# A fused attention and feed-forward kernel: the last piece of q is cut at another row, and the last three blocks run their steps in another order

## The chip, the cores and the metric

The kernel runs on one core of a Trainium2 chip. The metric is device time in microseconds (us), the median of several executions; before the change it is 696.37 us (four runs, 696.32 to 696.72). One execution was also profiled.

The core's engines work side by side, each through its own queue of instructions in order: TensorE (PE in the profile, PEld for its weight loads) multiplies matrices into PSUM, VectorE (DVE) and ScalarE (ACT) work elementwise, GpSimd (POOL) here mostly issues transfers, SyncE (SP) issues transfers only. They wait for each other through semaphores.

## What is computed

Cross-covariance attention per batch (4 batches, 6080 tokens, 256 channels): q and k are normalised over the tokens, a 256 x 256 matrix of scores goes through a softmax, and its product with v passes through a feed-forward network with a hidden width of 2048 and the tanh form of GELU.

```python
def _attn_ref(q, k, v, tau):
    qn = q / (np.linalg.norm(q, axis=1, keepdims=True) + 1e-06)
    kn = k / (np.linalg.norm(k, axis=1, keepdims=True) + 1e-06)
    s = kn.transpose(0, 2, 1) @ qn / tau
    s = s - s.max(-1, keepdims=True)
    a = np.exp(s)
    a /= a.sum(-1, keepdims=True) + 1e-09
    return (v @ a).astype(np.float32)

def _moe_ref(x, w_in, w_out):
    h = x @ w_in
    c = np.float32(np.sqrt(2.0 / np.pi))
    g = 0.5 * h * (1.0 + np.tanh(c * (h + 0.044715 * h * h * h)))
    return (g @ w_out).astype(np.float32)
```

## The kernel before

**Start.** Batch 0's q and k come in six chunks of up to 8 rows (a row is 128 tokens of 256 channels). For each row TensorE adds to the Gram matrix of q and k (`gram_row`, L248) and to the sums of squares (`ss_rows`, L269 for q, L275 for k), of squares that ScalarE or VectorE forms (`square`, `square_rows`, L203 and L205). The last chunk is loaded in five transfers from POOL's queue, listed in `PIECES` as (0 for q or 1 for k, first row, row after the last). After it come eight filler matmuls (`warm`, L370), the transposition of the first block of v, and the scores (`scores`), from which the combined matrix aw = (attention times w_in) is formed.

**Blocks.** The tokens of all batches are cut into 48 blocks (n = 0 to 47) of 512 tokens; the last of each batch, so block 47 too, has 448. For a block, h = aw times v is formed, GELU gives g, and w_out times g is the output. Both products save multiplications with a scheme of sums and seven half-size products, so that many small sums stand between the matmuls. In a block of the last batch:

- `g0`, `g3`: plain products for pairs 0 and 3 of the hidden units (`mm1`, L521); `G0`, `G3` their GELU on ScalarE (L531).
- Three sets, 0 to 2, of the scheme for the first product. `w0m6` is product 6 of set 0 (`small`, L597). Its sums and GELUs are in `set_step`: `cq` and `y5` are copies on ScalarE (L613, L616), `ap` and `ax` sums on VectorE (L618, L621), `Gq`, `Gx`, `Gr` the GELUs (L623, L631, L628). Product m6 accumulates on the bank that `cq` reads, and m7 needs the sum `ap`.
- `vs`: sums of the next block's v (L559 to L562, VectorE).
- `T1a` to `T4b`: sums of g for the second product (L687, L699, L701, L703, VectorE); `M1A` to `M7B` are its products, four matmuls each (`product`, L726). They accumulate in two banks, r (M1, M6, M7, M4) and p (M5, M3, M2); in block 47 M2 has a bank s of its own.
- `cq`, `y5`, `y6` without a set: copies of r and p to SBUF on ScalarE (`keep`, L736). `ap`, `ax`, `c11a`, `a12`: sums on VectorE (L776, L742). `c11`, `c12`, `c21`, `c22`: transposition of the four quarters of the output on VectorE (`turn`, L751). `ax` reads r before M4 adds to it; `c11a` needs M2, `c21` M4, `c12` M3.
- A block is stored when its fourth quarter is turned (`store`, L816): four transfers from SP's queue, in block 46 two from SP and two from POOL. Block 47 is stored in halves (`store_half`, L804): `sB` after `c11` and `c21`, `sA` after `c12` and `c22`, each in two transfers from SP and two from ScalarE's queue, in turn.

**Order.** Nothing reorders these steps: `ORDER` is a list of strings, written out, and each engine's queue gets its instructions in the sequence of the steps. A suffix -1 or +1 means the block before or after. `WINDOW` gives each block its string; the last four strings serve blocks 44, 45, 46 and 47 alone.

```python
        for n in range(NN):
            for x in ORDER[WINDOW[n]].split():
                m = re.match(r"([A-Za-z]+\d*[A-Za-z]*\d?)(?:([+-])(\d+))?$", x)
                step(m[1], n + {None: 0, "+": 1, "-": -1}[m[2]] * int(m[3] or 0))
```

Transfers from SP and ScalarE signal through eight semaphores that the build deals out in turn; before a transfer uses one, its queue waits until the transfer that had it before has landed. Transfers from POOL have eight of their own.

Of the kernel before, what the change touches and what calls it, by code (L numbers as in the profile page):

```python
# [18 lines left out]
def kernel(  # L19
# [55 lines left out]
    def chunks_of(b):  # L75
        sizes = [8, 7, 8, 8, 8, 8] if b == 0 else [6, 6, 6, 6, 6, 6, 6, 5]
        assert sum(sizes) == R
        res, r0 = [], 0
        for n in sizes:
            res.append((r0, n))  # L80
            r0 += n
        return res
# [48 lines left out]

    PIECES = [(0, 0, 4), (1, 0, 5), (1, 5, 8), (0, 4, 6), (0, 6, 8)]

    def load_last():
        c = len(chunks_of(0)) - 1
# [2 lines left out]
        qk_tiles[0, c] = [qkp.tile([128, 8, 256], BF16, tag="qk"[w], name=f"last{w}") for w in range(2)]  # L140
        for w, a, e in PIECES:
            nc.gpsimd.dma_start(
# [26 lines left out]
    def rows_of(b, c):  # L169
        r0, n = chunks_of(b)[c]  # L170
        rows = [(r, 128) for r in range(n)]
        if with_rest(b, c):
            rows.append((n, REM))
        return rows

    def new_squares(b, c):
        sq = sqp.tile([128, 8, 512], BF16, tag="sq", name=f"sq{b}_{c}")
        if with_rest(b, c):
            nc.vector.memset(sq[REM:, chunks_of(b)[c][1], :], 0.0)
        SQ[b, c] = sq  # L180
# [16 lines left out]
    def square_rows(c, which, a, e, eng):  # L197
        if (0, c) not in SQ:
            new_squares(0, c)
        t = qk_tiles[0, c][which][:, a:e, :]  # L200
        o = SQ[0, c][:, a:e, which * 256 : which * 256 + 256]
        if eng == "act":
            nc.scalar.activation(o, t, AF.Square)  # L203
        else:
            nc.vector.tensor_mul(o, t, t)  # L205
# [34 lines left out]
    def gram_row(b, c, i):  # L240
        first = b not in G
        if first:
            G[b] = pM.tile([128, 2, 256], FP32, tag="a", name=f"G{b}")
        qt, kt = qk_tiles[b, c]
        rows = rows_of(b, c)
        r, np_ = rows[i]
        for jc in range(2):
            nc.tensor.matmul(  # L248
                G[b][:, jc, :],
                lhsT=qt[:np_, r, jc * 128 : jc * 128 + 128],  # L250
                rhs=kt[:np_, r, :],
                start=first and jc == 0, stop=jc == 1,
                skip_group_check=True)

    def ss_rows(c, which, rows=None):


        last = c == len(chunks_of(0)) - 1
        n = SQR.get((0, c), 8)
        rows = range(n) if rows is None else rows  # L260
        if c == 0:
            SS[which] = pM.tile([128, 2] if which == 0 else [128, 256], FP32,
                                tag="sp"[which], name=f"ss0{which}")
        sq = SQ[0, c]
        for r in rows:
            end = last and r == n - 1
            if which == 0:
                for jc in range(2):
                    nc.tensor.matmul(SS[0][:, jc : jc + 1],  # L269
                                     lhsT=sq[:, r, jc * 128 : jc * 128 + 128],  # L270
                                     rhs=ones_bf[:, 0:1],
                                     start=c == 0 and r == 0 and jc == 0,
                                     stop=end and jc == 1)
            else:
                nc.tensor.matmul(SS[1], lhsT=ones_bf, rhs=sq[:, r, 256:512],  # L275
                                 start=c == 0 and r == 0, stop=end)
# [544 lines left out]
    with tc.manual_schedule():  # L821
# [42 lines left out]
        c = nch - 1  # L864
# [6 lines left out]
        ss_rows(c, 0, range(0, 4))  # L871
        ss_rows(c, 1, range(0, 5))
        square_rows(c, 1, 5, 8, "dve")
        square_rows(c, 0, 4, 6, "dve")
        ss_rows(c, 1, range(5, 8))
        for i in (4, 5):
            gram_row(0, c, i)
        ss_rows(c, 0, range(4, 6))
        square_rows(c, 0, 6, 8, "dve")
        for i in (6, 7):  # L880
            gram_row(0, c, i)
        ss_rows(c, 0, range(6, 8))
        wi = moe_w_in.rearrange("(c p) d -> p c d", p=128)
        load_v0(0)
        for f0, f1 in ((0, 256), (256, 512), (512, 1024), (1024, 1536), (1536, 2048)):
# [293 lines left out]
    w1Gr T4b-1 w2m7 G3 w2m3 w2ax M2A-1 w2m2 ax-1 M2B-1 w2Gq T4a-1 w2m4""",  # L1179
    """g0 T1a-1 w2Gr-1 w1m1 G0 M4A-2 c11a-2 w0m5 w0m1 T3a-1 M4B-2 w0cq M5B-1 c21-2 w0y5 w1m5  # L1180
    T2a-1 w0m6 w2Gx-1 M5A-1 w0ap M1A-1 w1y5 M1B-1 T2b-1 w1cq w0m7 cq-1 w0m2 w0ax w0m3 y5-1
    w1m6 w0Gq M6A-1 w1ap w0m4 M6B-1 lt+3 T3b-1 w0Gr w1m7 w2m5 ap-1 w1m2 w2y5 w1m3 vs+1 w2m1
    M3A-1 w2cq w1ax M3B-1 w1Gq M7B-1 c12-1 w2m6 c11-2 M7A-1 w1Gx w2ap w1m4 w0Gx g3 c22-2 w1Gr
    T4b-1 w2m7 G3 w2m3 w2ax M2A-1 w2m2 ax-1 M2B-1 w2Gq T4a-1 w2m4""",
    """g0 T1a-1 w2Gr-1 w0m5 w1m1 w0y5 w0m1 c11a-2 M4A-2 T3a-1 w0cq M4B-2 G0 M5B-1 c21-2 w0m6
    M5A-1 w0ap w2Gx-1 w1m5 T2a-1 w1cq w0m7 w0m3 w1y5 w0m2 w0ax w1m6 M1A-1 w0Gq w1ap w0m4 M1B-1
    T2b-1 w0Gr w1m7 w2m5 T3b-1 cq-1 w1m3 w2m1 y5-1 M6A-1 w1ax w2cq M6B-1 w2y5 w1m4 ap-1 w2m6
    w0Gx w1m2 w2ap M3A-1 w1Gq M3B-1 vs+1 w2m7 M7B-1 w1Gr w2ax w2m3 w1Gx w2m2 c12-1 M7A-1 w2Gq
    c11-2 w2m4 g3 c22-2 T4b-1 w2Gr w0m5+1 ax-1 G3 M2A-1 T4a-1 M2B-1 w0m1+1 c11a-1""",
    """g0 w0cq T1a-1 w0y5 w0m6 M4A-2 G0 w0ap M4B-2 M5B-1 T2a-1 w2Gx-1 w1m5 w0m7 c21-2 w1y5 w1m1  # L1190
    w0ax w0m2 w0m3 w1cq M1B-1 T2b-1 w0Gq M1A-1 T3a-1 M5A-1 cq-1 w1m6 c11-2 w0m4 y5-1 w2m5 w1ap
    w0Gr M6B-1 T3b-1 M6A-1 w2y5 w2m1 ap-1 w1m7 w2cq w1m2 T4b-1 w1m3 M7B-1 w1Gq c22-2 w2m6 w1ax
    M3B-1 M3A-1 w2ap w1Gx g3 vs+1 w0Gx w2m7 c12-1 G3 w2m2 w2m3 w2ax M7A-1 M2A-1 w2Gq ax-1 w2m4
    T1a w1m4""",
    """g0 w2Gr-1 w1Gr-1 w0m5 T4a-2 w0m1 M2B-2 w0y5 T2a-1 M4B-2 w0cq M4A-2 c11a-2 G0 c22-2 w0m6
    w1m1 c21-2 M5B-1 w2Gx-1 w0ap w1m5 M1B-1 w1cq T3a-1 M1A-1 w1y5 T2b-1 w0m7 w0m2 cq-1 w0m3
    w0ax w1m6 M5A-1 w0Gq w1ap M6B-1 y5-1 w0m4 T3b-1 M6A-1 w0Gr w2m5 w1m3 ap-1 w1m2 w2y5 T4a-1
    w2m1 w1m7 M7A-1 w2cq T4b-1 M3B-1 w1Gq c11-2 M3A-1 w1ax w2m6 M7B-1 w2ap w1Gx g3 ax-1 w0Gx
    c12-1 w2m7 w2m3 G3 c22-1 M4B-1 w2ax w2m2 M2B-1 T1a w2Gq M4A-1 M2A-1 w2Gx c21-1 w1m4 w2m4
    c11a-1 M1B w2Gr c11-1 M1A w1Gr T2a M5B cq M5A T2b M6A T3a M6B M2B T3b y6 y5 T4b M7A M7B  # L1200
    T4a M3A ax M2A M4B c11a M4A c11 M3B c21 a12 sB c12 c22 sA""",
]


# [33 lines left out]
```

## Time and profile before

| what | value |
|---|---|
| median of four runs | 696.37 us |
| the profiled execution | 696.32 us |
| its span, first to last instruction | 694.5 us |
| TensorE busy | 672.3 us, 97% |
| VectorE busy | 630.8 us, 91% |
| ScalarE busy | 616.2 us, 89% |
| granted TensorE clock, mean | 0.999 |
| chain that ended last, share of TensorE | 94% |
| chain that ended last, share of transfers | 4% |

The page gives the busy time of each engine, the span in slices, the transfers by queue, and the chain of work that ended last: it starts at the last instruction of an engine and goes back, at each step to whatever released it. Further views list the chain in order of time, the instructions of a stretch (start, duration, engine, line, what is written and read, how often, and in brackets the idle time before and what ended it), the waits by pair of engines, and the busy time in stretches. SPq and ACTq are the queues that issue transfers.

### The profile page before, as it was taken

What the parts mean: (1) busy time and instruction counts of PE and PEld (TensorE: products, weight loads), DVE (VectorE), ACT (ScalarE), POOL (GpSimd) and SP (SyncE); (2) the same over time, 40 slices, a digit from 0 to 9 for tenths busy, and PEclk for the clock granted to TensorE, in tenths of its full rate; (3) what the DMA queues carried; (4) which work ended last, traced back from release to release, by engine and by line L of the source; (5) the groups of instructions that cost most, each with busy time, mean ns of one, the idle gap of its engine ahead of it and who ended that gap; (6) DMA issues with size and microseconds to landing.
All of it is one profiled execution on the core that took longest, in us unless ns stands there. A gap on an engine that the chain in (4) does not pass through costs nothing.

```text
span 694.5 us, 14338 instructions
## 1 busy us (share of the span) xinstructions
PE 672.3 (97%) x5426; PEld 531.0 (76%) x5501; DVE 630.8 (91%) x1245; ACT 616.2 (89%) x894; POOL 73.4 (11%) x135
## 2 busy tenths in 40 slices
PE   4999999999999999999999999999999999999996
PEld 2757787777778777777777777777777888888785
DVE  4489998999998989999999889999999999999996
ACT  5389989999889999998888999999888999999993
POOL 4321101101011001101010110010000000000000
PEclk9999999999999999999999999999999999999999
DMA  9996887896478766747577777683563463463325
GB/s 242 208 269 99 161 142 122 120 148 108 70 138 131 135 113 111 114 80 126 88 137 120 119 126 124 95 139 55 81 99 69 77 103 61 82 102 59 54 39 89
DMA packets 161462, 79.07 MB, mean 114 GB/s; under 512 B 148448, under 2 KB 152160, under 8 KB 160672
## 3 DMA queue, kind: packets, MB, share of 16 engines
q0 software_dynamic: 14448, 39.72, 34.0%
q1 hardware_dynamic: 145696, 37.14, 32.0%
q10 hardware_dynamic: 1248, 1.28, 0.6%
q8 instruction: 43, 0.70, 0.4%
q14 instruction: 27, 0.22, 0.1%
HBM read 78.91 MB, written 36.57 MB: 166 GB/s over the span
## 4 chain that ended last, share of the span: by engine, by line
PE 94%; DMA 4%; issue 1%; ACT 0%; DVE 0%; POOL 0%; DVEq 0%; POOLq 0%; ACTq 0%
PE r L726 24%; PE h L521 21%; PE p L726 18%; PE rb L597 13%; PE qp L597 10%; PE G L248 5%; DMA t<-in_k_dram 2%; PE awp L461 2%; DMA t<-in_q_dram 1%; PE ss L282 0%; PE ss L275 0%; PE vt_ps L325 0%; PE rk L406 0%; PE warm L370 0%; DVE vT_pe L331 0%
## 5 line engine op out<-in xcount | busy, mean ns | idle before, releaser
L726 PEld LDWEIGHTS <-wcomb 128*128 128x128 bf16 x2688 | 262.2, 98 | 43.2 <-issue 0.2
L531 ACT ACTIVATE g<-h 128x1024 bf16<-128x1024 f32 (+1 forms) x178 | 180.0, 1014 | 16.3 <-PE h L521 13.7
L726 PE MATMUL r<-t,wcomb 128*128 128x256 bf16 (+1 forms) x1152 | 163.5, 271 | 0.1
L521 PE MATMUL h<-vT,aw 128*128 128x512 bf16 (+1 forms) x560 | 153.6, 376 | 3.5
L623 ACT ACTIVATE g<-qp 128x1024 bf16<-128x1024 f32 (+1 forms) x103 | 104.6, 1016 | 7.2 <-PE qp L597 5.8
L726 PE MATMUL p<-g,wcomb 128*128 128x256 bf16 (+1 forms) x760 | 108.0, 272 | 0.0
L521 PEld LDWEIGHTS <-aw 128*128 128x128 bf16 x712 | 69.3, 98 | 49.3 <-DVE aw L364 0.6
L597 PEld LDWEIGHTS <-sw 128*128 128x128 bf16 x824 | 80.3, 98 | 25.5 <-issue 1.3
L193 ACT ACTIVATE sq<-t 128x1536 bf16<-128x1536 bf16 (+4 forms) x59 | 79.2, 1358 | 8.3 <-DMA t<-in_q_dram 8.3
L618 DVE TENSOR_TENSOR qp<-rb,yw 128x512 f32<-128x512 f32 (+1 forms) x103 | 70.9, 688 | 12.3 <-PE rb L597 9.4
L597 PE MATMUL rb<-tv,sw 128*128 128x256 bf16 (+1 forms) x412 | 77.9, 271 | 0.3 <-DVE qp L618 0.2
L621 DVE TENSOR_TENSOR xw<-rb,yw 128x512 f32<-128x512 f32 (+1 forms) x103 | 69.5, 675 | 3.9 <-PE rb L597 2.4
L613 ACT ACTIVATE qp<-rb 128x512 f32<-128x512 f32 (+1 forms) x103 | 59.7, 580 | 11.9 <-PE rb L597 6.8
L597 PEld LDWEIGHTS <-aw 128*128 128x128 bf16 x618 | 60.3, 98 | 12.7 <-issue 0.7
L631 ACT ACTIVATE g<-xw 128x512 bf16<-128x512 f32 (+1 forms) x103 | 63.4, 626 | 1.3 <-DVE xw L621 1.2
L616 ACT ACTIVATE yw<-qp 128x512 f32<-128x512 f32 (+1 forms) x103 | 61.2, 594 | 3.7 <-PE qp L597 1.9
L699 DVE TENSOR_TENSOR t<-g,t 128x1024 bf16<-128x1024 bf16 (+1 forms) x96 | 63.5, 668 | 0.6
L701 DVE TENSOR_TENSOR t<-g 128x1024 bf16<-128x1024 bf16 (+1 forms) x96 | 63.9, 674 | 0.0
L703 DVE TENSOR_TENSOR t<-t,g 128x1024 bf16<-128x1024 bf16 (+1 forms) x96 | 63.6, 670 | 0.0
L628 ACT ACTIVATE g<-rb 128x512 bf16<-128x512 f32 (+1 forms) x103 | 61.2, 596 | 2.2 <-PE rb L597 1.7
L248 PE MATMUL G<-t 128*128 128x256 bf16 (+1 forms) x352 | 58.9, 275 | 0.8 <-DMA t<-in_k_dram 0.8
L687 DVE TENSOR_TENSOR t<-g 128x2048 bf16<-128x2048 bf16 (+1 forms) x48 | 57.5, 1198 | 0.0
(137 smaller groups left out, 888.1 us busy)
## 6 DMA issues: line engine op xcount, KB each, us to landing
out_dram<-ot SPq DMA_DIRECT2D x174, 128.0 KB, 3.2
vb<-in_v_dram POOLq DMA_DIRECT2D x41, 256.0 KB, 4.1
t<-in_q_dram POOLq DMA_DIRECT2D x21, 384.0 KB, 4.7
t<-in_k_dram POOLq DMA_DIRECT2D x21, 384.0 KB, 6.1
wst<-in_moe_w_out_dram POOLq DMA_DIRECT2D x2, 1024.0 KB, 11.2
t<-in_q_dram POOLq DMA_DIRECT2D x3, 512.0 KB, 15.1
t<-in_k_dram POOLq DMA_DIRECT2D x3, 512.0 KB, 16.9
out_dram<-ot SPq DMA_DIRECT2D x12, 112.0 KB, 2.5
```

The costliest lines, as they stand in the source:

```text
L193: nc.scalar.activation(o, t[:np_, r, :], AF.Square)
L248: nc.tensor.matmul(G[b][:, jc, :], lhsT=qt[:np_, r, jc * 128 : jc * 128 + 128], rhs=kt[:np_, r, :], start=first and jc == 0, stop=jc == 1, ...
L521: mm = nc.tensor.matmul(hp[:, u, :cols], lhsT=AW[b][:, cc, fc * 128 : fc * 128 + 128], rhs=vt_tiles[n][:, cc, :cols], start=cc == 0, stop= ...
L531: nc.scalar.activation(gs(n)[:, 2 * p : 2 * p + 2, :cols], HP.pop((n, p))[:, :, :cols], AF.Gelu_apprx_tanh)
L597: GATE[0] = nc.tensor.matmul(acc[:, u * hc : u * hc + hc], lhsT=lhs[:, u * 128 : u * 128 + 128], rhs=rhs, start=m in (1, 5) and u == 0, st ...
L618: nc.vector.tensor_add(qp(n, i)[:, 1, :c], RB[n, i][:, :c], YW[n, i][:, :c])
L621: nc.vector.tensor_add(XW[n, i][:, :c], RB[n, i][:, :c], YW.pop((n, i))[:, :c])
L623: nc.scalar.activation(gs(n)[:, 2 * pa : 2 * pa + 2, :c].rearrange("p u (t x) -> p t u x", t=2), QP.pop((n, i))[:, :, :c].rearrange("p t ( ...
L699: nc.vector.tensor_sub(o, quarter(n, 1, 1, f0, f1), ts[1][:, f0:f1, :hc])
L701: nc.vector.tensor_sub(o, quarter(n, 1, 1, f0, f1), quarter(n, 0, 1, f0, f1))
L703: nc.vector.tensor_sub(o, ts[2][:, f0:f1, :hc], quarter(n, 1, 0, f0, f1))
L726: nc.tensor.matmul(ACCS[n, acc][:, :hc], lhsT=wcomb[:, w, fc, :], rhs=x, start=first and k == 0, stop=k == 3, skip_group_check=True)
```

## The change

There are two edits. In the last chunk of batch 0, the last two transfers of q, rows 4 to 5 and 6 to 7, become rows 4 to 6 and row 7; the squares, Gram matmuls and norms follow that cut. The number of transfers, squares and matmuls stays.

In the order of the steps, block 44's string moves `w1ax` ahead of `vs+1`, and the strings of blocks 45, 46 and 47 are replaced. The steps are the same in number and kind over these blocks together; some move from one string to another (a step of block 45 that stood in the string of block 46, for instance).

```diff
-    PIECES = [(0, 0, 4), (1, 0, 5), (1, 5, 8), (0, 4, 6), (0, 6, 8)]
+    PIECES = [(0, 0, 4), (1, 0, 5), (1, 5, 8), (0, 4, 7), (0, 7, 8)]
...
-        square_rows(c, 0, 4, 6, "dve")
+        square_rows(c, 0, 4, 7, "dve")
         ss_rows(c, 1, range(5, 8))
-        for i in (4, 5):
+        for i in (4, 5, 6):
             gram_row(0, c, i)
-        ss_rows(c, 0, range(4, 6))
-        square_rows(c, 0, 6, 8, "dve")
-        for i in (6, 7):
-            gram_row(0, c, i)
-        ss_rows(c, 0, range(6, 8))
+        ss_rows(c, 0, range(4, 7))
+        square_rows(c, 0, 7, 8, "dve")
+        gram_row(0, c, 7)
+        ss_rows(c, 0, range(7, 8))
...
-    w1m6 w0Gq M6A-1 w1ap w0m4 M6B-1 lt+3 T3b-1 w0Gr w1m7 w2m5 ap-1 w1m2 w2y5 w1m3 vs+1 w2m1
-    M3A-1 w2cq w1ax M3B-1 w1Gq M7B-1 c12-1 w2m6 c11-2 M7A-1 w1Gx w2ap w1m4 w0Gx g3 c22-2 w1Gr
+    w1m6 w0Gq M6A-1 w1ap w0m4 M6B-1 lt+3 T3b-1 w0Gr w1m7 w2m5 ap-1 w1m2 w2y5 w1m3 w1ax w2m1
+    M3A-1 w2cq vs+1 M3B-1 w1Gq M7B-1 c12-1 w2m6 c11-2 M7A-1 w1Gx w2ap w1m4 w0Gx g3 c22-2 w1Gr
     T4b-1 w2m7 G3 w2m3 w2ax M2A-1 w2m2 ax-1 M2B-1 w2Gq T4a-1 w2m4""",
-    """g0 T1a-1 w2Gr-1 w0m5 w1m1 w0y5 w0m1 c11a-2 M4A-2 T3a-1 w0cq M4B-2 G0 M5B-1 c21-2 w0m6
-    M5A-1 w0ap w2Gx-1 w1m5 T2a-1 w1cq w0m7 w0m3 w1y5 w0m2 w0ax w1m6 M1A-1 w0Gq w1ap w0m4 M1B-1
-    T2b-1 w0Gr w1m7 w2m5 T3b-1 cq-1 w1m3 w2m1 y5-1 M6A-1 w1ax w2cq M6B-1 w2y5 w1m4 ap-1 w2m6
-    w0Gx w1m2 w2ap M3A-1 w1Gq M3B-1 vs+1 w2m7 M7B-1 w1Gr w2ax w2m3 w1Gx w2m2 c12-1 M7A-1 w2Gq
-    c11-2 w2m4 g3 c22-2 T4b-1 w2Gr w0m5+1 ax-1 G3 M2A-1 T4a-1 M2B-1 w0m1+1 c11a-1""",
-    """g0 w0cq T1a-1 w0y5 w0m6 M4A-2 G0 w0ap M4B-2 M5B-1 T2a-1 w2Gx-1 w1m5 w0m7 c21-2 w1y5 w1m1
-    w0ax w0m2 w0m3 w1cq M1B-1 T2b-1 w0Gq M1A-1 T3a-1 M5A-1 cq-1 w1m6 c11-2 w0m4 y5-1 w2m5 w1ap
-    w0Gr M6B-1 T3b-1 M6A-1 w2y5 w2m1 ap-1 w1m7 w2cq w1m2 T4b-1 w1m3 M7B-1 w1Gq c22-2 w2m6 w1ax
-    M3B-1 M3A-1 w2ap w1Gx g3 vs+1 w0Gx w2m7 c12-1 G3 w2m2 w2m3 w2ax M7A-1 M2A-1 w2Gq ax-1 w2m4
-    T1a w1m4""",
-    """g0 w2Gr-1 w1Gr-1 w0m5 T4a-2 w0m1 M2B-2 w0y5 T2a-1 M4B-2 w0cq M4A-2 c11a-2 G0 c22-2 w0m6
-    w1m1 c21-2 M5B-1 w2Gx-1 w0ap w1m5 M1B-1 w1cq T3a-1 M1A-1 w1y5 T2b-1 w0m7 w0m2 cq-1 w0m3
-    w0ax w1m6 M5A-1 w0Gq w1ap M6B-1 y5-1 w0m4 T3b-1 M6A-1 w0Gr w2m5 w1m3 ap-1 w1m2 w2y5 T4a-1
-    w2m1 w1m7 M7A-1 w2cq T4b-1 M3B-1 w1Gq c11-2 M3A-1 w1ax w2m6 M7B-1 w2ap w1Gx g3 ax-1 w0Gx
-    c12-1 w2m7 w2m3 G3 c22-1 M4B-1 w2ax w2m2 M2B-1 T1a w2Gq M4A-1 M2A-1 w2Gx c21-1 w1m4 w2m4
-    c11a-1 M1B w2Gr c11-1 M1A w1Gr T2a M5B cq M5A T2b M6A T3a M6B M2B T3b y6 y5 T4b M7A M7B
-    T4a M3A ax M2A M4B c11a M4A c11 M3B c21 a12 sB c12 c22 sA""",
+    """g0 T1a-1 w2Gr-1 w0m5 G0 M4A-2 c11a-2 w0m1 w1m1 T3a-1 M4B-2 w0cq w1m5 w0y5 c21-2 w0m6 M5B-1
+    w2Gx-1 w0ap M5A-1 w1cq T2a-1 w0m7 w1y5 w0m2 w0m3 w0ax w1m6 w0Gq M1A-1 w1ap w0m4 M1B-1
+    T2b-1 w0Gr w1m3 w1m7 cq-1 w2m5 w1ax w2m1 y5-1 M6A-1 w2cq T3b-1 M6B-1 w2y5 w1m2 ap-1 w2m6
+    w0Gx w1m4 w2ap M3A-1 w1Gq M3B-1 vs+1 w2m2 w2m3 w1Gr c12-1 w2m7 g3 w2Gq c11-2 c22-2 w2ax
+    M7B-1 G3 M7A-1 T4b-1 w2m4 w0m5+1 ax-1 w2Gr M2A-1 T4a-1 M2B-1 w0y5+1 T1a w0m1+1 w2Gx""",
+    """g0 w0cq M4A-2 c11a-2 G0 T2a-1 w0m6 w1m1 M4B-2 w0ap w1Gx-1 w1m5 M5A-1 T3a-1 w1cq w0m7 w0m2
+    w1y5 w0ax w0m3 M5B-1 w0Gq c21-2 w1m6 w0m4 c11-2 M1A-1 w1ap w0Gr w2m5 M1B-1 T3b-1 w2y5 w2m1
+    w1m2 cq-1 T2b-1 w1m7 w2cq w1m3 M6A-1 w1ax w1Gq w2m6 M6B-1 T4a-1 w1m4 y5-1 w2ap g3 w0Gx
+    ap-1 w2m7 vs+1 G3 M7A-1 w2m2 w2ax M3B-1 w1Gr M3A-1 T4b-1 w2Gx w2m3 M7B-1 c12-1 w1Gx c22-2""",
+    """g0 w2Gq-1 T1a-1 w2m4-1 M2A-2 w2Gr-1 M2B-2 ax-2 T3a-1 w0m5 w1m1 G0 w0m1 c11a-2 M4B-2 T2a-1
+    M4A-2 w0cq M5A-1 w0y5 c22-2 c21-2 w0m6 w1m5 M5B-1 w0ap w1cq M1B-1 T2b-1 w1y5 M1A-1 T3b-1
+    w0m7 w1m6 cq-1 w0m2 w0ax y5-1 w0m3 M6A-1 w0Gq w1ap M6B-1 w0m4 w1m3 ap-1 w1m2 w0Gr T4a-1
+    w2m5 M7B-1 w1Gq c11-2 w2m1 w1m7 T4b-1 M3B-1 w2cq M7A-1 w1ax w2y5 w2m6 g3 ax-1 w1Gx w2ap
+    w0Gx M3A-1 c22-1 G3 w2m7 w2m2 c12-1 w2m3 w2ax M4B-1 w2Gq M4A-1 T1a w2m4 w2Gx M2A-1 w1m4
+    w2Gr c21-1 M2B-1 T2a w1Gr M1A c11a-1 M1B T2b M5A cq T3a M6A T3b M6B M5B c11-1 y6 T4a y5
+    M7A T4b M7B M2A ax M2B M4A c11a M4B c11 M3A c21 M3B sB a12 c12 c22 sA""",
```

## The prediction

> **What bounds the kernel now.** I read the page first (what is busy), then the busy time of the last stretches, then the chain of waits at both places that the change touches, then the queues at the very end. Two lines of the page:
>
> ```profile
> span 694.5 us, 14338 instructions
> PE 672.3 (97%) x5426; PEld 531.0 (76%) x5501; DVE 630.8 (91%) x1245; ACT 616.2 (89%) x894; POOL 73.4 (11%) x135
> ```
>
> TensorE is busy 97% of the span, so elsewhere a new order can only win back TensorE's gaps. The profiled execution took 696.32 us, 1.8 us more than its span; the median of the four runs is 696.37. Sums below are made against the span and carried to the median as differences. From the table of stretches:
>
> ```profile
> 670.00:680.00 10.00, 10.00 (x93) 8.77 (x92) 9.74 (x20) 9.17 (x17) 0.00 (x0) 1.00 0.07 12
> 690.00:694.50 4.50, 0.00 (x0) 0.00 (x0) 0.00 (x0) 0.00 (x0) 0.00 (x0) 0.81 0.47 82
> ```
>
> After the width come busy time and count of TensorE, its weight loads, VectorE, ScalarE, POOL, then clock and DMA. TensorE has no gap from 670 to 680, VectorE 0.26 us. After 690 no engine computes: 4.5 us belong to the stores of the last block alone.
>
> The first place, the last piece of q (the chain of waits, then VectorE's row from the timeline):
>
> ```profile
> 33.43 0.44 PE G L248 x4
> 33.87 0.08 PE ss L269 x4
> 33.95 0.46 PE G L248 x4
> 34.41 0.08 PE ss L269 x4
> 34.48 0.90 PE warm L370 x8
> ...
> 33.41 0.42 DVE L205 TENSOR_TENSOR sq<-last 128x512 bf16<-128x512 bf16 x1 [0.29 <-DMA last<-in_q_dram]
> ```
>
> The chain runs on TensorE without a break: rows 4 and 5, their norms, rows 6 and 7, theirs, the filler. The piece is squared from 33.41 to 33.83, while TensorE reaches its norms at 34.41.
>
> The second place, the start of block 45 (chain of waits, then a row of the timeline with the idle time of the weight loads):
>
> ```profile
> 647.82 0.23 PE rb L597 x2
> ...
> 648.14 0.71 DVE qp L618
> 648.85 0.04 issue
> 648.89 0.38 PE rb L597 x2
> ...
> 648.89 0.31 PEld L597 LDWEIGHTS <-sw 128*128 128x128 bf16 x3 [0.38 <-issue]
> ```
>
> Product w0m6 ends, VectorE forms the sum w0ap (L618), and only then can w0m7 run. TensorE stands 0.38 us: the longest gap in the last four blocks.
>
> The end (chain of waits; then the waits of SP's queue and rows of the timeline):
>
> ```profile
> 684.38 0.78 PE r L726 x8
> 685.16 0.02 issue
> 685.19 0.37 ACT y L736
> 685.55 0.04 issue
> 685.60 0.93 PE r L726 x8
> ...
> SPq L804 <- DMA out_dram<-ot: 1.8, 1, 1.8
> 688.54 0.38 ACTq L804 DMA_DIRECT2D out_dram<-ot  x1
> 690.65 0.32 SPq L804 DMA_DIRECT2D out_dram<-ot  x1
> 686.55 1.36 POOL L816 DMA_DIRECT2D out_dram<-ot  x2 [59.53 <-issue]
> ```
>
> The last block's half sB is stored as soon as c21 is turned (688.51): SP and ACT each issue at 688.54. SP's second store of sB is issued only at 690.65, because in the program it signals through the same semaphore as ACT's first store, which lands 2.1 us after its issue. SP's stores of sA stand behind it (691.07, 691.51; ready since 689.6), and the span ends at 694.5. So the end is fixed by the turn of c21: issue of sB, call it t0 = 688.54, plus 5.97 us. TensorE's own end (688.44) has over a microsecond to spare.
>
> **The change part by part.** *The piece of q.* The five transfers move the same bytes; rows 4 to 6 come in one, row 7 alone. The transfer of rows 4, 5 was issued at 18.19 and landed 14.5 us later (32.7); that of rows 6, 7 at 20.65, 12.7 later (33.35). Three rows land midway, about 33.0, before TensorE asks (33.43); row 7 lands at 33.35 and is asked for at 33.43 + 6 x 0.11 + 0.12 = 34.2. Squares: three rows are 0.49 (the 128x768 form on this line), so 33.05 to 33.55; one row alone is not in the trace, between 0 and the 0.42 of two rows, so done by 33.97 at the latest; its norms are asked for at 34.4. The matmuls are the same 16. Everything is hidden under TensorE, and the eight filler matmuls (0.90) lie between it and the next real work. One POOL issue, moe_w_out's first half, waits for the piece of rows 4 to 6: from 33.26 to at most 33.35, and nothing behind it is short. Price 0, bounds -0.1 and +0.1 (the rest of the cover is a few tenths; without it TensorE would wait for row 7, 0.1).
>
> *Block 44* only moves w1ax ahead of the sums vs+1 on VectorE (0.68 against about 1.0): no wait of TensorE hangs on either there. 0.
>
> *Block 45.* In the old order 4 + 2 matmuls (M5A, w1m5) lie between w0m6 and w0m7, 6 x 0.109 = 0.65; in the new one M5B and M5A, 8 x 0.109 = 0.87. The wait of 0.38 shrinks by 0.22, and the copy w0cq, now behind the GELU G0 on ACT (0.91 from start to start), finishes about when w0m6 wants it: a new wait between 0 and 0.2. Price -0.15, bounds -0.38 and +0.1.
>
> *Block 47, the product of its own tail.* Old sequence on TensorE (groups of four matmuls at 0.093 = 0.37): M1 M1 M5 M5 M6 M6 M2, wait, M7 M7 M3 M2 M4 M4 M3. New: M1 M1 M5 M6 M6 M5, wait, M7 M7 M2 M2 M4 M4 M3 M3. Two effects. First, M6 accumulates on the bank that ACT copies after M1. M1's results come 0.18 after its last issue, the copy takes 0.36, handing over about 0.1: 0.62 in all, and only one group (0.37) covers it where two did (0.75). New wait 0.24. The wait before M7 (0.24 from the end of M2 at 685.36 to 685.60) stays, with M5B as cover in place of M2B. M7 then starts after 0.75 + 0.37 + 0.24 + 0.75 + 0.37 + 0.24 = 2.72 us from M1 instead of 2.91 measured: 0.19 earlier. Second, M4 now comes before both halves of M3, so c21 need not wait for M3A: between M7 and the end of M4 there are still six groups (M7, M2, M4 against M7, M3A, M2A, M4), so this gives nothing on TensorE. VectorE must have done ax before M4 begins: T4 ends at 686.60, ax at 687.02, and M4 would want to begin at 685.41 + 1.50 = 686.91. If VectorE is not earlier than now, M4 begins at 687.07, ends at 687.82, results at 688.00, c21 turns from 688.03: 0.06 before its present 688.09. If VectorE comes earlier too (it stood 0.28 and 0.23 us near 648 for TensorE), the whole 0.19. I take -0.1, bounds -0.4 and +0.3. M3B ends some 0.3 later than now; that moves sA's data to 689.9, still ahead of SP's 691.07.
>
> *The store of block 46.* The last turn, c11-1, moves behind four more VectorE instructions (L699 and L701, two each, 683.33 to 685.5): 2.1 us later. SP's two stores of it go from 683.44 to about 685.5; the slower landed 3.8 us after its issue, so 689.4, across t0. POOL's two stores of the same block follow on the same turn: now they start at 686.55, 3.1 us after it, although other POOL issues start 0.3 after their release. The row bounds the new start: 0.3 after the turn is 685.8, 3.1 after it is 688.6. VectorE's T4 end (686.6) fits the old start to 0.05, so I take "about where it was". Price 0 to +0.3 by shared transfers, I take +0.1; the far end is a rival below.
>
> What held POOL for 3.1 us is open. VectorE ran nothing but two-input sums in SBUF between the turn and T4's end (L699, L701, L703), but a transfer of POOL at 601.68 began in the middle of an L701 (601.45 to 602.13). The Trainium skill (SBUF — State Buffer, "Who interferes with whom") says of just this form that it takes only the read half of the ports shared with POOL and was not seen to hold up POOL's transfers. By that rule the coincidence with T4's end is none, POOL's start goes with the turn, and this speaks against the change: the sum would be that of rival 3 if the 3.1 us go along. By the coincidence it would be +0.
>
> Queues: SP and ACT keep their sequence of stores. The semaphores are dealt differently: SP's second sB store still waits for ACT's first (the 1.8 us stay), and SP's first sA store now waits for ACT's second, issued 0.42 later and landing by the time SP gets there. 0, at most +0.2.
>
> Sum: 0 + 0 - 0.15 - 0.1 + 0.1 + 0 = -0.15 us, 696.2.
>
> **The rivals.** (1) *Nothing moves.* VectorE's end decides M4, the won gap near 648 is given back at the waits inside block 47: 696.3 to 696.5. For it: VectorE has only 0.26 us of idle time in 670 to 680. (2) *The gaps all go.* The 0.38 near 648, 0.09 at 653 and 0.24 at 685 vanish and c21 comes a group (0.37) earlier: at most -1.1, 695.3. Against it: the copy before M7 is unchanged. (3) *Slower: the late store of block 46 collides with sB.* Place: the transfers after 688.5. If POOL's store starts 3.1 us after the turn, its 0.26 MB lie wholly after t0 (now some 0.06 MB are moved by 688), beside the remainder of SP's; at the 164 GB/s that this stretch of stores reached, 0.06 to 0.16 MB more are 0.4 to 1.0 us. It decides once ACT's first sB store takes over 2.1 + 0.2 us, since SP's queue stands on that landing: 696.6 to 697.4. For it: the 3.1 us of the row. (4) *Row 7 in front*: bounded by 0.1, no case of its own.
>
> **How the numbers follow.** A measurement here tells 0.2% (1.4 us) from no change. Forecast, a small gain of 0 to 0.5: chance 0.50, own range 695.8 to 696.35. Rival 1: 0.20. Rival 2: 0.13. Rival 3: 0.17. No term reaches 1.4 us by itself; for faster than 694.98 rival 2 would need more gaps than there are (0.03), for slower than 697.76 rival 3 its far end and a lost gap as well (0.08). Within: 0.89. Range: 695.5 to 697.1, from most of rival 2 to most of rival 3.
>
> **What would show it.** In the profile after: no change in the chain from 33.4 to 36.6; the wait of w0m7 at block 45 near 0.2; a new TensorE wait of about 0.24 after M1 of block 47; sB issued at 688.3 to 688.5 and SP's second store 2.1 later; POOL's store either near 686.6 or near 688.6. The prediction is wrong if SP's queue no longer stands on ACT's landing, or if a wait of over half a microsecond appears on TensorE in blocks 45 to 47.

## The result, and the profile after

| | before | after |
|---|---|---|
| median | 696.54 us (51 runs, 696.18 to 697.21) | 697.73 us (31 runs, 697.27 to 699.04) |
| ratio of the times | 1 | 1.0018, 95% interval 1.0013 to 1.0023 |
| profiled execution | 696.32 us, span 694.54 us | 697.76 us, span 695.92 us |
| first store of block 47 issued (sB) | 688.54 | 688.65 |
| from there to the landing of the last store | 4.74 us | 6.00 us |
| from that landing to the end of the span | 1.27 us | 1.26 us |

The kernel became 1.2 us slower, and the prediction (696.2 us, 695.5 to 697.1) was wrong. The table already says where: from the issue of the first store of block 47 to the landing of the last it takes 1.26 us more than before. The page of the kernel after:

```profile
span 695.9 us, 14340 instructions
PE 673.5 (97%) x5426; PEld 531.3 (76%) x5501; DVE 630.5 (91%) x1245; ACT 616.0 (89%) x894; POOL 73.5 (11%) x135
```

Counts and busy times are those of before to within 1.2 us; the engines do the same work.

The first place, the piece of q. The chain of waits of the kernel after (start, duration, what):

```profile
33.76 0.66 PE G L248 x6
34.42 0.13 PE ss L269 x6
34.54 0.24 PE G L248 x2
34.78 0.03 PE ss L269 x2
34.81 0.90 PE warm L370 x8
```

TensorE still runs without a break, now 6 + 2 instead of 4 + 4. All of it stands 0.33 us later than in the profile of before, and so does everything ahead of it from 28.3 us on, where the large chunk of k lands (28.59, before 28.26). Most of that is a difference between executions: in the 16 profiles of this study the norms that follow start anywhere from 30.2 to 31.1 us. (The four with the old cut of q start at 30.2 to 30.5, the twelve with the new one at 30.2 to 31.1, so a small part of the new cut isn't excluded by the starts alone.) So times near the end are compared below as distances from the first store of block 47, or in two profiles with the same start.

The second and third place, blocks 45 and 47. Rows of the timeline of the kernel after, with the idle time of the weight loads in brackets:

```profile
649.16 0.10 PEld L597 LDWEIGHTS <-sw 128*128 128x128 bf16 x1 [0.29 <-issue]
...
684.34 1.15 PEld L726 LDWEIGHTS <-wcomb 128*128 128x128 bf16 x12 [0.22 <-issue]
685.71 2.97 PEld L726 LDWEIGHTS <-wcomb 128*128 128x128 bf16 x31 [0.22 <-issue]
```

The wait ahead of w0m7 shrank from 0.38 to 0.29, there is a new wait after M1 and M5 in block 47, and the one ahead of M7 stayed.

The end, in the kernel after: the waits of SP's queue (us in total, times, longest), POOL's row of the timeline, and ScalarE's second store of sB among the transfers (its last column is the time from issue to landing):

```profile
SPq L804 <- DMA out_dram<-ot: 3.2, 2, 1.8
```

```profile
688.70 1.36 POOL L816 DMA_DIRECT2D out_dram<-ot  x2 [61.34 <-DVE ot L751]
```

```profile
out_dram<-ot ACTq DMA_DIRECT2D x1, 56.0 KB, 3.4
```

The same store in the kernel before:

```profile
out_dram<-ot ACTq DMA_DIRECT2D x1, 56.0 KB, 1.9
```

POOL's two stores of block 46 now start at 688.70, with sB, where they started at 686.55. And SP waits twice for a landing, 3.2 us, where it waited once, 1.8 us.

How busy the transfers are from 684 to 696 us, in 40 slices of 0.3 us (each digit tenths of the 16 DMA engines), first before, then after:

```profile
DMA  0899996100006793949994855858640010000000
```

```profile
DMA  0000100079879910006987999968793659100000
```

Before, the first part of block 46 moves from 684.3 to 686.4, then from 687.6 on block 46's rest and block 47 follow without a gap to 693. After, the first part moves from 686.4 to 688.5, nothing moves for 0.9 us, and the rest and block 47 begin together at 689.4 and end at 694.5. The 0.26 MB of POOL's stores have moved out of a time with room into the time that sets the end.

### The profile page after: what moved, and what is told of

It reads as the page before. It is cut to its first block, busy times and chain, and to the rows that moved or that the text cites. A ratio compares the mean times of both kernels' runs of the same rounds, so it can differ in the third digit from the quotient of the medians.

```text
span 695.9 us, 14340 instructions
## 1 busy us (share of the span) xinstructions
PE 673.5 (97%) x5426; PEld 531.3 (76%) x5501; DVE 630.5 (91%) x1245; ACT 616.0 (89%) x894; POOL 73.5 (11%) x135
## 3 DMA queue, kind: packets, MB, share of 16 engines
q10 hardware_dynamic: 1248, 1.28, 0.6%
## 4 chain that ended last, share of the span: by engine, by line
PE 94%; DVE 1%; ACT 1%; DMA 1%; issue 1%; SPq 0%; DVEq 0%; ACTq 0%
PE r L726 23%; PE h L521 21%; PE p L726 17%; PE rb L597 13%; PE qp L597 9%; PE G L248 6%; PE awp L461 2%; DMA qk_f<-in_q_dram 1%; PE warm L370 1%; PE ss L275 1%; PE ss L282 0%; ACT sq L193 0%; PE ss L269 0%; PE vt_ps L325 0%; DVE qp L618 0%
```

## The experiments

The theory after this reading: the late turn of block 46 puts POOL's stores beside the last block's, which land later; and a store of SP that shares a semaphore with a slowed one waits for it. The rivals were the rest of the order, the new dealing of the semaphores, and the piece of q. The 95% interval of each ratio below reaches some 0.6 to 0.7 us to either side. For each run the table gives the median beside that of the kernel before on the same chip, when POOL's stores of block 46 start and when the last store lands, both counted from the first store of block 47.

| run | median | before beside it | POOL's store starts | last landing |
|---|---|---|---|---|
| before | 696.54 | | -1.99 | 4.74 |
| after | 697.73 | 696.54 | +0.05 | 6.00 |
| e1_piece | 696.54 | 696.58 | -2.00 | 4.70 |
| e1_order | 697.57 | 696.58 | +0.06 | 5.81 |
| e1_before_late | 698.09 | 696.58 | +0.02 | 6.21 |
| e1_after_early | 697.21 | 696.58 | -1.43 | 5.39 |
| e2_after_free | 696.20 | 696.64 | -2.79 | 4.07 |
| e2_after_sp46 | 696.60 | 696.64 | none | 4.87 |
| e2_early_free | 696.16 | 696.64 | -4.27 | 4.04 |
| e2_before_free | 696.28 | 696.64 | -4.84 | 3.83 |
| e3_touch | 698.66 | 696.65 | +0.06 | 6.91 |
| e3_held | 697.51 | 696.65 | +0.27 | 5.55 |
| e3_tail | 695.92 | 696.65 | -4.58 | 3.78 |
| e4_wake_load | 698.52 | 696.64 | +0.08 | 6.90 |
| e4_wake41 | 696.90 | 696.64 | -2.79 | 4.80 |
| e4_tail_pool | 696.25 | 696.64 | -4.57 | 4.08 |

### One part alone

*The piece.* The kernel before with the diff's first half (`PIECES` and the lines that follow it).

> The kernel before with the new cut of q's last piece alone. Theory (the loss lies in the late store of block 46): nothing changes, 696.5, within 0.15 us of the kernel before. Rival (the piece is part of the loss: in the profile after, the whole run from 34 us on lies 0.33 us later than before): +0.3 us, and the filler matmuls begin near 34.8 because TensorE waits for a piece of q.

Ratio 0.9999 (0.9990 to 1.0007): no cost of the piece shows. Its profile begins 0.47 us late as well, and yet its median is that of before, which is why the start is put down to the execution; a cost of a few tenths would lie within the interval.

*The order.* The kernel before with the diff's second half.

> The kernel before with the new order alone. Theory: all of the loss, +1.0 to +1.3 us (697.5 to 697.9); sB issued at 688.3 to 688.6, ACT's second store of sB taking over 3 us, the end 7.2 us after the issue of sB where it was 5.97. Rival (piece): +0.9 at most, 0.3 short of the kernel after.

Ratio 1.0016 (1.0007 to 1.0024): the loss of the whole change, within the intervals. This profile has the same start as that of before (norms at 30.21 in both), so it can be laid over it: block 47's first product starts at 682.62 against 682.69, M7 at 685.37 against 685.60, and sB is issued at 688.31 against 688.54. The order wins 0.23 us up to the first store and loses 1.07 after it.

*The late turn alone.*

```diff
-    c11a-1 M1B w2Gr c11-1 M1A w1Gr T2a M5B cq M5A T2b M6A T3a M6B M2B T3b y6 y5 T4b M7A M7B
+    c11a-1 M1B w2Gr M1A w1Gr T2a M5B cq M5A T2b M6A T3a M6B M2B T3b c11-1 y6 y5 T4b M7A M7B
```

> The kernel before, with one step moved: the last turn of block 46 stands behind the last sum of T3 in block 47, some 1.6 us later, as in the kernel after. Theory: POOL's two stores start 3.1 us after the turn, near 688.2, ACT's second store of sB takes about 3 us in place of 1.9, and a store of sA from SP stands on its landing (here the second, through the same semaphore): +0.6 to +1.3 us. Rival A (the loss is in the rest of the order, its new wait on TensorE and its other semaphores): within 0.2 us of the kernel before. Rival B (what holds POOL's stores is VectorE's run of sums): POOL's first store starts where it did, near 686.6, and the time stays.

Ratio 1.0021 (1.0012 to 1.0030). One moved turn makes the kernel before lose as much as the whole change does (by the medians more, 1.5 against 1.2 us, but the intervals overlap). Its last turn of block 46 and POOL's stores:

```profile
685.03 0.44 DVE L751 STREAM_TRANSPOSE ot<-c 128x256 f32<-128x256 f32 x1
688.60 1.36 POOL L816 DMA_DIRECT2D out_dram<-ot  x2 [61.54 <-DVE ot L751]
```

TensorE's order is that of before, and POOL starts at 688.60, 3.13 us after the end of the turn (685.47), not near 686.6: rivals A and B both fall.

*The turn moved back.*

```diff
-    w2Gr c21-1 M2B-1 T2a w1Gr M1A c11a-1 M1B T2b M5A cq T3a M6A T3b M6B M5B c11-1 y6 T4a y5
+    w2Gr c21-1 M2B-1 T2a w1Gr M1A c11a-1 c11-1 M1B T2b M5A cq T3a M6A T3b M6B M5B y6 T4a y5
```

> The kernel after, with one step moved back: the last turn of block 46 stands right behind the sum c11a, some 2 us earlier. Theory: the stores of block 46 are out of the way, the end comes 6.0 us after the issue of sB again; 696.3 to 696.6, which is 1.1 to 1.4 us below the kernel after. The semaphores are dealt as in the kernel after, so if these alone are the cause, or the order's wait on TensorE (rival A), it stays at 697.3 to 697.8.

697.21, ratio 1.0007 (0.9998 to 1.0016): about half came back, less than expected. With 3.13 us from turn to store POOL starts 1.43 us ahead of sB, where the kernel before has 1.99, and its second store still lands 2.3 us behind the issue of sB: the collision is smaller, not gone.

### The late store and the shared semaphores apart

These kernels change who issues the stores of blocks 45 and 46. With two of block 45's on POOL, SP has two fewer, and the dealing of the eight semaphores moves on.

```diff
-            eng = nc.gpsimd if n == NN - 2 and bi > 1 else nc.sync
+            eng = nc.gpsimd if n in (NN - 3, NN - 2) and bi > 1 else nc.sync
```

That is e2_after_free; e2_early_free has the early turn too, e2_before_free is the same edit in the kernel before, and e2_after_sp46 has `n == NN - 3` in place of the pair.

> The kernel after, with the last two of block 45's four stores moved from SP's queue to POOL's. This shifts the dealing of the semaphores: SP's stores of sB and the first of sA no longer share one with a store of ScalarE's queue (the second of sA shares with ScalarE's first of sB). POOL's stores of block 46 stay as late as they are. Theory (the late store of block 46 slows the transfers, and SP's wait on a slowed one passes it on): SP issues without a wait, at 688.65, 689.05, 690.1, 690.5; about 0.7 MB move after 688.65 at some 164 GB/s, last landing near 693.2, 1.2 to 1.6 us below the kernel after: 696.0 to 696.6. Rival (bandwidth alone: the end is when all bytes are moved): not below 697.3. Second question, what holds POOL's stores for 3.1 us: if it is the 61 us for which POOL had nothing to do, block 46's first store now starts within 1 us of its turn (near 686.2); if it belongs to each such store, it stays 3.1.

> The kernel after, with block 46 stored from SP's queue alone (four stores from 685.6 on) and the last two of block 45's stores from POOL's in exchange, so that SP's stores of sB and sA share semaphores with ScalarE's as in the kernel after: its second of sB waits for ScalarE's first, its first of sA for ScalarE's second. Theory: the collision is gone, ScalarE's second store lands 2 us after its issue, SP's first of sA is issued near 691.2, the end comes 6.0 us after the issue of sB: 696.3 to 696.6. Rival (the dealing of the semaphores alone): the wait of SP stays and so does the time, 697.4 or more.

> The kernel after, with both: the last turn of block 46 early, right behind the sum c11a, and two of block 45's stores from POOL's queue, so that SP's stores wait for none of ScalarE's. Theory: less collides and nothing waits, 695.6 to 696.2, below the kernel before by 0.4 to 1.0. Rival (bandwidth alone): as the early turn alone, 697.2.

> The kernel before, with two of block 45's stores from POOL's queue: the 1.8 us for which SP stood on the landing of ScalarE's first store are gone. Theory: SP issues at 688.5, 688.9, 689.65, 690.0; the last store lands 0.9 to 1.3 us earlier than now (693.28): 695.3 to 695.7. Rival (the wait only covers time in which the transfers are busy anyway): 696.4 to 696.6, no change.

Ratios 0.9993, 0.9999, 0.9993 and 0.9994, each with an interval of about 0.0009 to either side. The loss is gone in the three that start from the kernel after. In e2_after_sp46 block 47's semaphores are shared as in the kernel after and the late store is gone, and the time is that of before within the interval, the last landing too (4.87 and 4.74 us): no cost of the dealing alone shows. In e2_after_free the late store went away by itself, which had been the second question. POOL's rows of its timeline:

```profile
681.02 1.37 POOL L816 DMA_DIRECT2D out_dram<-ot  x2 [53.81 <-DVE ot L751]
685.70 1.29 POOL L816 DMA_DIRECT2D out_dram<-ot  x2 [3.31 <-DVE ot L751]
```

Block 45's store starts 3.13 us after its turn (677.89), block 46's 0.29 after its own (685.41). So this run doesn't tell collision and wait apart. e2_before_free fell short of its expectation: the last landing came 0.91 us earlier, as expected, but the time only 0.36. Most of the rest went behind the landing (last section). There POOL's stores of block 46 start 2.85 us earlier as well, so the 0.91 are not the price of the shared semaphore alone.

*The fourth corner.* Of the four combinations of a late or early store with shared or separate semaphores, the kernel after is late and shared, e2_after_sp46 early and shared, e2_after_free early and separate. Late and separate is left: the dealing of e2_after_free, with POOL's two stores held back. Its core:

```diff
+            if n == NN - 2 and bi == 1:
+                HELD.append((dst, ot, cols))
+                break
...
+            if last and what == "c21":
+                store_held()
```

`store_held` issues a small copy on POOL that reads block 47's output, and then the two stores.

> The fourth corner: semaphores dealt so that SP waits for none of ScalarE's landings that matter (two of block 45's stores on POOL), but POOL's two stores of block 46 held back on purpose, behind a small copy that waits for the turn c21 of block 47, so that they start near 688.8 as in the kernel after. If the collision costs by itself: 697.0 or more, nearly the kernel after. If it costs only through SP's wait on the slowed landing: 696.1 to 696.6. I expect between, nearer the second: ScalarE's second store of sB slow (over 3 us), SP's stores issued without delay, 696.3 to 696.9.

697.51, ratio 1.0013 (1.0004 to 1.0022): nearly the kernel after, so the collision costs by itself, and the guess of its size was wrong. SP hardly waits (0.6 us), ScalarE's second store of sB takes only 2.4 us (issued 0.16 us behind POOL's first, 0.37 in the kernel after); it is the four stores of sA that land late. Those of SP and ScalarE issued at 690.5:

```profile
out_dram<-ot SPq DMA_DIRECT2D x1, 56.0 KB, 3.5
out_dram<-ot ACTq DMA_DIRECT2D x1, 56.0 KB, 3.7
```

### Why POOL starts late

*A small copy on POOL ahead of it*, in the kernel after:

```diff
         TS.setdefault(n, {})[1] = t1
+        if n == NN - 1:
+            scr = const.tile([128, 8], BF16)
+            nc.gpsimd.tensor_copy(scr, t1[:, 0, 0:8])
```

> The kernel after, with one small addition: POOL copies 8 elements per partition of block 47's first sum (T1a) to a scratch tile that nothing reads. Its last work before that is 55 us back. Stores, queues, order and semaphores are those of the kernel after. Theory (POOL is slow by 3.1 us at its first instruction after long idleness, whatever the instruction, and only then): the small copy starts some 3 us after T1a, block 46's first store from POOL 0.3 us after its turn, near 685.9 in place of 688.7; nothing collides with sB, the end comes 6.0 us after its issue: 696.3 to 696.6. Rival A (the 3.1 us belong to the first store, or to the first transfer, not to the idleness): POOL's store stays at 3.1 us after the turn and the time at 697.5 or more. Rival B (not the late store but the dealing of the semaphores): the store is early, the time stays.

*A small load ahead of it*: instead of the copy, `nc.gpsimd.dma_start(out=scr, in_=q[0, 0:128, 0:8])` behind the same sum.

> The kernel after, plus one small transfer on POOL's queue: 4 KB of q into a scratch tile that nothing reads, issued once block 47's first sum (T1a, done near 682.4) is formed. Semaphores and stores as in the kernel after. Theory now (a POOL transfer waits 3.1 us more when POOL has issued none for some 50 us; a small copy does not count): the small transfer starts 3.1 us after T1a, near 685.6, and the store of block 46 follows at once behind its turn, near 686.2 in place of 688.7. The store then lies before sB, and the loss of the late store goes: 696.3 to 696.8, at least 0.8 below the kernel after. Rival A (the delay belongs to POOL's first store, loads are free of it): the small transfer starts 0.3 us after T1a, the store stays at 3.1 us after its turn, 697.5 or more. Rival B (the semaphores carry the loss): the store is early and the time stays at 697.4 or more.

*A store 52 us ahead of it*: `n in (41, NN - 2)` in the line of the stores.

> The kernel after, with two of block 41's stores on POOL as well, some 3 us behind POOL's last load (626.9) and 55 us ahead of block 46's. If the delay comes with the time without a transfer: block 41's store starts about 0.3 us after its turn, block 46's 3.1 us, and the time stays at 697.4 to 698.0. If it belongs to the first store: the reverse, and the time falls to 696.3 to 696.8.

POOL's rows of the three timelines, copy, load, store:

```profile
682.97 0.19 POOL L691 COPY scr<-t 128x8 bf16<-128x8 bf16 x1 [55.10 <-DVE t L687]
689.20 1.37 POOL L819 DMA_DIRECT2D out_dram<-ot  x2 [6.04 <-DVE ot L754]
```

```profile
682.62 0.57 POOL L691 DMA_DIRECT2D scr<-in_q_dram  x1 [55.34 <-DVE t L687]
688.65 1.34 POOL L819 DMA_DIRECT2D out_dram<-ot  x2 [5.46 <-DVE ot L754]
```

```profile
633.94 1.37 POOL L816 DMA_DIRECT2D out_dram<-ot  x2 [6.62 <-DVE t L703]
685.81 1.29 POOL L816 DMA_DIRECT2D out_dram<-ot  x2 [50.50 <-DVE ot L751]
```

Copy and load start at once after 55 us without work, and the store behind them is still late (689.20 for a turn that ended at 686.06). Block 41's store starts 3.14 us after its turn (630.80) though POOL had loaded 7 us before, and block 46's, 50 us later, without delay. So idleness isn't it, and my theory was wrong in both runs: the delay goes with POOL's first store in the program.

e4_wake41 is also the cleanest test of the loss. Order, turn and sharing of semaphores among block 47's stores are those of the kernel after; POOL's start moved from +0.05 to -2.79. (The last store also signals through another semaphore, which by the last section adds 0.45 us behind its landing.) Its transfers from 684 to 696 us, without the gap of the kernel after and done by 693:

```profile
DMA  0000020089799998589995085999580000000000
```

The time fell from 1.19 above the kernel before to 0.26 above it (ratio 1.0003, 0.9995 to 1.0012). e3_touch and e4_wake_load, on the contrary, were 0.7 to 0.8 us slower still than the kernel after, each counted from the kernel before beside it: ScalarE's second store took 4.3 us to land, SP's first store of sA stood on it (4.0 us of waits), and in e4_wake_load the transfers stand idle from 693.3 to 693.9 for want of an issue:

```profile
DMA  1000100099899600009999999958695001957000
```

So the shared semaphore can add to a collision; without one (e2_after_sp46, e4_wake41) no loss of it shows against the kernel before. Why ScalarE's store took 4.3 us here and 3.4 in the kernel after is not shown; the kernel after itself has executions of up to 699.04, and none of these was profiled.

### A faster kernel

Two tries put the findings together: two stores of block 45 and three of block 46 on POOL, the early turn, and in block 47 a sequence in which two groups of matmuls run while each copy of a bank is made, and sA is stored first.

```diff
-    w2Gr c21-1 M2B-1 T2a w1Gr M1A c11a-1 M1B T2b M5A cq T3a M6A T3b M6B M5B c11-1 y6 T4a y5
-    M7A T4b M7B M2A ax M2B M4A c11a M4B c11 M3A c21 M3B sB a12 c12 c22 sA""",
+    w2Gr c21-1 M2B-1 T2a w1Gr M1A c11a-1 c11-1 M1B T2b M5A cq T3a M5B M6A T3b M6B y5 M2A y6 T4a
+    M2B T4b M7A c11a M7B c11 M3A ax M3B c22 M4A a12 M4B c12 sA c21 sB""",
```

> A try at a faster kernel: the kernel after with (1) two of block 45's and three of block 46's stores on POOL, so that POOL is awake and SP waits for no landing, (2) the turn of block 46 early, (3) block 47's last products as M1 M1 M5 M5 M6 M6 M2 M2 M7 M7 M3 M3 M4 M4, so that each copy of a bank is covered by two groups, and sA stored before sB. VectorE is then the bound of the end: seven steps of 0.35 to 0.4 us behind T4. The first half is ready near 688.8, the second near 689.1 to 689.3 where it is 690.1 in the kernel after: 695.2 to 695.9. If the transfers are the bound instead (0.45 MB of block 47 and the rest of block 46 at 164 GB/s), 695.9 to 696.3. Theory of the copies wrong: 696.2 or more.

> The try at a faster kernel, with POOL's queue as a third one for block 47's stores: sA from SP, ScalarE, POOL, SP and sB from ScalarE, POOL, SP, ScalarE. The last issue comes near 690.1 in place of 690.7. If the issues bound the end: 0.2 to 0.5 us below the try before it (695.92), 695.4 to 695.7. If the transfers bound it, or POOL's store lands later than the queues' own: no gain, 695.9 to 696.2.

e3_tail: 695.92, ratio 0.9990 (0.9981 to 0.9999): faster than both kernels, by 0.7 us and, each counted from the kernel before beside it, 1.9 us. It lies between the two ranges that were expected, and which of its parts won the time was not tried. With POOL as a third queue it is 696.25 (0.9994, 0.9986 to 1.0003): the issues end 1 us after the first instead of 1.4, yet the last store lands 4.08 us after it instead of 3.78, so earlier issues won nothing here.

## Why the prediction was wrong, step by step

- *Piece of q, price 0*: right within the interval, by the run of it alone.
- *Block 44, 0*: nothing speaks against it; it was not tried alone.
- *Block 45, wait 0.38 less 0.22 to near 0.2*: the wait is 0.29, the gain 0.07 to 0.09 where 0.15 was taken. The direction was right.
- *Block 47, new wait 0.24 after M1, the wait before M7 stays, c21 0.06 to 0.19 earlier*: right. The new wait reads 0.22, and with block 45 together the first store is issued 0.23 earlier (predicted 0.25). The later end of M3B, called harmless, was so: e4_wake41 has it, and its last store lands 4.80 us after the first, against 4.74.
- *Semaphores, 0*: right for the dealing, with e2_after_sp46 and e4_wake41. That ScalarE's second store lands "by the time SP gets there" was not so in the kernel after: SP stood 1.4 us more, as that store was slowed (next point).
- *The store of block 46, "about where it was", +0.1*: this step failed. Two rows bounded POOL's start: 686.6, because VectorE's T4 ended there, or 688.6, 3.1 us after the turn. I took the coincidence with T4. POOL's first store starts 3.13 to 3.16 us after its turn in all 16 profiles, in the kernel after at 688.70, while T4 ended at 686.61. So the term was taken at +0.1 where the stretch behind the first store of block 47 grew by 1.26 us. The rule cited against that choice, the Trainium skill (SBUF — State Buffer, "Who interferes with whom"), that two-input sums in SBUF were not seen to hold up POOL's transfers, agrees with these 3.13 to 3.16 us: it was the better guide than one coincidence.

Rival 3 had the mechanism and the place, but its size and the store it was to be told by were off. It counted the bytes, 0.06 to 0.16 MB more after the issue of sB, for 0.4 to 1.0 us. That count was right as far as it goes: in the kernel before half of POOL's 0.26 MB moves after the issue of sB, in the kernel after all of it, 0.13 MB more. But nothing of sB itself moves in the first 0.8 us after its issue. In the kernel before POOL's bytes fill that time, and 0.47 MB move after it; in the kernel after it stands empty, and 0.73 MB move after it. So the stretch that sets the end got the whole 0.26 MB more. At the 164 GB/s that the rival used this would be 1.6 us by estimate; measured were 1.26. And it was to be decided by ScalarE's first store, which landed in 2.1 us as before; the slow one was the second (3.4), issued 0.4 us later and so behind POOL's.

The sum, with what the runs showed: 0 for the piece, -0.23 up to the first store, and +1.26 from there to the last landing, by the two profiles 1.03 us, against 1.19 by the medians.

Left open: the price of the two late stores with nothing else moved. Kernels that leave them out, planned for this, gave no time; the least disturbed measures are e4_wake41, and e3_held against e2_after_free (5.55 and 4.07 us to the last landing).

## What to carry to other kernels

Where a moved step releases a store, follow the store's bytes to where they land, and ask what the transfers do just before the end: a store that filled idle time may cost its whole length when it slides into the last block's. Where two rows bound a start and lie far apart, as 686.6 and 688.6 did here, a coincidence of one profile is no reason to take the cheap one; move the releasing step in the head and see which of the two readings moves along. And a queue's first store may start late, as POOL's did in every profile here: let it happen early, where nothing waits for it.

## What the runs showed of the hardware

- POOL's first store starts 3.13 to 3.16 us after its release in all 16 profiles, a later one that finds POOL free 0.29. A load or a copy ahead doesn't take it away, an earlier store does, even 50 us earlier. Why is open; in e4_wake41 no transfer of instructions is recorded between 628 and 636 us, around the delay.
- A store of 56 KB of block 47 lands 1.7 to 2.1 us after its issue in the kernel before. In the six runs in which POOL's two 128 KB stores of block 46 start with sB or up to 0.3 us after it, those issued 0.3 to 1.9 us behind one of POOL's take 2.6 to 4.3 us, those issued ahead of POOL's or within 0.2 us 1.8 to 2.4, and those issued 2.9 us behind or later 1.7 to 1.8. The distance alone doesn't decide it: in the kernel before stores issued 1.3 us behind POOL's second take 1.7 and 2.1 us.
- From the last landing to the end of the span it is 1.26 to 1.28 us where the last store signals through the third of the eight semaphores, in the order in which the end of the program waits for them (nine profiles), and 1.71 to 1.73 us where it is the first (four); the other three, on the fourth to sixth, have 1.38 to 1.55. That is 0.45 us between the first and the third, and with it e2_before_free (0.47 of the missing 0.55 us) and e4_wake41 come out near what their landings promised. Why is open.
